# Batch 0's q in quarters and its k in pieces, k's maxima negated as they are written, identity products on TensorE, and a new order of all steps

## The chip, the cores and the metric

One core of a Trainium2 chip runs the kernel. Its engines work side by side, each through its own list of instructions in order: TensorE (PE for matmuls, PEld for loading their weights), VectorE (DVE), ScalarE (ACT), GpSimd (POOL), and SyncE (SP), which here issues every DMA. The metric is the device time of one execution in microseconds (us); less is better.

## The reference

Eight batches go through a linear attention and a gated MLP. Cut to what matters:

```python
q_s = softmax(q, axis=-1)              # q, k, v: (8 batches, 8 heads, 576 rows, 64)
k_s = softmax(k, axis=2)               # over the 576 rows
x   = q_s @ (k_s^T @ v)                # heads side by side: (8, 576, 512)
h   = gelu_tanh(x @ w_in)              # 512 -> 1024
u, v2 = h[..., :512], h[..., 512:]
v_n = (v2 - mean) / sqrt(var + 1e-6) * g_ln
v_s = w_sg @ v_n + b_sg                # over the 576 rows
out = x + (u * v_s) @ w_out
```

Both softmaxes take the maximum off before the exponential. w_in and w_out reach the device as 64-bit floating point.

## The kernel before, in words

All work is cut into named steps, one small Python function each. `PLAN` is one long text with about 1,270 steps such as `kv_mm 0 1` (batch 0, half 1) or `wi_a 3 G` (chunk 3, on GpSimd); the last loop of `gmlp_kernel` calls them in that order. `InOrder` chains each engine's instructions, so **each engine works through its own part of the plan strictly in order**, and so does SP with the DMAs. Engines meet only through data: a reader waits for the writer, and a writer into a buffer for its last reader. The planned order is thus the whole schedule, and a trailing letter (V, A, G) picks the engine.

A matmul on full fp32 would be slow, so each large operand is split in a high and a low part in the fp32r format, and a product is three matmuls (high x high, low x high, high x low).

- **Weights** (w_in in eight chunks `wi_* f`, w_out in four `wo_* f`): `load`, then `_a` (scale, ACT or POOL), `_b` (shift left by 3), `_c` (or the sign), `_d` (or the low word), all three on DVE, then `_h` (ACT rounds the high part) and `_l` (the low part). A low part comes either by a subtraction (DVE or POOL), or by `wi_x`, which lets TensorE form value minus high part with `eye` and `minus` (the identity and its negative) into PSUM, from where ACT copies it. w_sg goes the same way with `ws_h`, `ws_x`, `ws_l`.
- **k of a half of a batch**: for batch 0 it lies transposed (`TURN`), and `kr_max` takes the maxima over the rows with one reduction on DVE and negates them with a second small operation; `kr_exp` is the exponential on ACT, `ktr_mm` turns the result with ten transposes on TensorE, `kr_copy` and `kr_rest` bring it to `kk`. For the other batches `k_ma`, `k_mb`, `k_mc` fold the rows, further steps spread the maximum, `k_sub` and `k_exp` follow.
- **q of a half**: for batch 0 (`FLAT`) `qf_max`, `qf_sub`, `qf_exp`, `qf_sum`, `qf_inv` on a whole half, `qf_mul` on a quarter, then `qtr_mm` (transposes on TensorE) and `qf_copy` for each quarter. For the others `q_max`, `q_swapm`, `q_top`, `q_sub`, `q_exp`, `q_sum`, `q_swapd`, `q_inv`, `q_mul`, `q_turn` (a DVE transpose).
- **Attention**: `kv_mm` (k^T v), `kv_inv` and `kv_scale` (the division), `x_mm` (two of a batch), `x_high` and `x_low` (the split of x; in batch 0 some with `x_neg`, which takes the high part off in PSUM).
- **MLP**: `hu_mm` and `hv_mm` (x @ w_in for u and v; in batch 0 in two parts, `_first` and `_second`), `hu_gelu`, `hv_gelu`, `hv_sq`, `hv_stat`, `hv_pow`, `hv_norm`, `hv_high`, `hv_low`, the `tail_*` steps for the last 64 rows, `sg_mm` (the product over the rows), `gate`, `gate_high`, `gate_low`, `out_mm`, `out_base`, `out_add`, `out_store`. The last quarter of the last batch is halved in `last_mm`, `last_add`, `last_store`.

Buffers that steps share set waits: `kk`, `vv` and `qq` have one slot for each half, so `load_k b h` waits until `kv_mm b-1 h` has read the slot. PSUM has three two-bank tiles (`ps2`) and two one-bank tiles (`ps1`), handed out in turn by `bank` in the order of the plan.

Of the kernel before, what the change touches and what calls it, by code (L numbers as in the profile page):

```python
# [38 lines left out]
kv_inv 0 0, kv_scale 0 0, x_mm 0 0, x_high 0 0, wi_c 2, qf_mul 0 1 0 G, qtr_mm 0 2, wi_d 2, wi_h 2, load_w_in 7, wi_a 7 G, load_k 1 0, wi_b 7
load_k 1 1, wi_c 7, x_high 0 1, x_neg 0 0, wi_x 2, x_low 0 0 A, kv_inv 0 1, qf_copy 0 2, load_w_in 6, wi_b 1, k_ma 1 1, load_w_out 1, x_neg 0 1  # L40
x_low 0 1 A, k_ma 1 0, ws_x 3, wi_c 1, wi_a 6, k_mb 1 1, ws_l 3 A, kv_scale 0 1, x_mm 0 1, load_b, wi_d 1, wi_h 1, load_q 1 0, x_high 0 2, wi_b 6
load_q 1 1, k_mc 1 1, wi_c 6, wi_x 1, wi_l 1 A, k_mb 1 0, wi_d 7, x_neg 0 2, hu_first 0 0, wi_l 2 A, x_low 0 2 A, q_max 1 0, q_swapm 1 0, wi_h 7
wi_d 6, kt_mm 1 1, hu_first 0 2, x_high 0 3, k_mc 1 0, kt_mm 1 0, k_top 1 1, q_top 1 0, load_w_in 4, q_sub 1 0 G, q_max 1 1, kb_mm 1 1, k_top 1 0
x_low 0 3, hu_second 0 2, k_sub 1 1 V, hu_second 0 0, wi_a 4, wi_h 6, wi_l 7 G, b_h, load_w_in 5, wi_a 5, q_exp 1 0, hu_first 0 1, wi_b 5, wi_b 4
wi_c 5, wi_d 5, q_swapm 1 1, wi_c 4, q_top 1 1, q_sub 1 1 G, load_w_out 2, wi_h 5, load_v 1 1, load_w_out 3, kb_mm 1 0, k_exp 1 1, wi_d 4, wi_h 4
wi_x 6, wi_l 6 A, hu_second 0 1, k_sub 1 0 V, q_sum 1 0, wi_l 5 G, kv_mm 1 1, kv_inv 1 1, kv_scale 1 1, k_exp 1 0, q_swapd 1 0, load_v 1 0, kv_mm 1 0
wi_l 4 V, kv_inv 1 0, wo_a 2, load_w_sg 2, hv_first 0 3, hv_second 0 3, wo_a 3 G, b_l V, q_inv 1 0, kv_scale 1 0, q_exp 1 1, load_w_sg 1, hu_gelu 0 2
load_w_out 0, q_sum 1 1, q_mul 1 0 0 G, q_turn 1 0, hv_first 0 0, hv_gelu 0 3, wo_a 1, wo_b 1, wo_a 0, wo_b 3, wo_b 2, wo_c 3, hv_second 0 0, ws_h 1
q_mul 1 0 1 G, hv_gelu 0 0 A, load_w_sg 4, ws_h 2, wo_b 0, wo_c 0, wo_d 0, hu_gelu 0 0, hv_first 0 1, hv_second 0 1, q_turn 1 1, ws_h 4, wo_c 1
hv_gelu 0 1 A, wo_c 2, x_mm 1 0, wo_d 3, hu_gelu 0 1, q_swapd 1 1, wo_d 1, q_inv 1 1, q_mul 1 1 0 G, q_mul 1 1 1 G, hv_sq 0 1, load_v 2 0, x_high 1 0  # L50
wo_d 2, wo_h 2, wo_l 2 G, hv_first 0 2, hv_second 0 2, x_low 1 0, q_turn 1 2, hu_first 0 3, x_high 1 1, load_q 2 0, x_low 1 1, hv_sq 0 0, hv_first 0 4
ws_l 2 G, hv_gelu 0 2 A, hv_sq 0 2, q_turn 1 3, x_mm 1 1, load_g, hv_norm 0 1, x_high 1 2, hu_second 0 3, hv_stat 0 0 A, hv_pow 0 0, hv_stat 0 3
x_low 1 2, hv_stat 0 1 A, hv_pow 0 1, x_high 1 3, x_low 1 3, load_v 2 1, hv_pow 0 3, hv_norm 0 3, hv_high 0 3, hv_norm 0 0, hv_stat 0 2 A, hv_pow 0 2
hv_low 0 3, hv_high 0 0, hv_low 0 0, hv_second 0 4, hv_gelu 0 4 A, load_k 2 0, hv_sq 0 4, k_ma 2 0, k_mb 2 0, hv_high 0 1, ws_l 1 V, hv_mm 1 2
hv_gelu 1 2 A, hv_norm 0 4, hv_stat 0 4 A, hv_pow 0 4, hv_norm 0 2, load_k 2 1, hu_gelu 0 3, hv_low 0 1, k_ma 2 1, tail_high 0, tail_low 0, k_mc 2 0
k_fold 2 0, hv_sq 1 2, hv_high 0 2, hv_low 0 2, tail_high 1, tail_low 1, hv_mm 1 1, k_rota 2 0, k_maxa 2 0, load_q 2 1, k_rotb 2 0, q_max 2 1, wo_h 3
wo_l 3 G, hv_stat 1 2 A, tail_again 0, ws_l 4 V, out_base 0 2 G, wo_h 1, k_maxb 2 0, hv_mm 1 0, hv_gelu 1 0 A, hv_pow 1 2, sg_mm 0 2, q_max 2 0
hv_gelu 1 1, hv_stat 1 1, hv_norm 1 1, hv_pow 1 1, gate 0 2, q_swapm 2 0, q_swapm 2 1, hv_sq 1 0, q_top 2 1, q_sub 2 1 V, sg_mm 0 0, k_sub 2 0 V
sg_mm 0 1, k_exp 2 0, q_top 2 0, k_mb 2 1, gate 0 1, gate_high 0 2, q_sub 2 0 V, q_exp 2 0, gate 0 0, gate_high 0 0, gate_low 0 0 G, sg_mm 0 3
gate_high 0 1, gate_low 0 1 G, hv_norm 1 2, hv_high 1 2, kv_mm 2 0, k_mc 2 1, k_fold 2 1, q_sum 2 0, q_swapd 2 0, gate 0 3, gate_high 0 3, q_inv 2 0  # L60
gate_low 0 2 V, hv_mm 1 3, q_exp 2 1, gate_low 0 3 G, q_mul 2 0 1 G, wo_h 0, out_base 0 3 V, q_sum 2 1, hv_stat 1 0 A, wo_l 0 V, hv_gelu 1 3
hv_stat 1 3, hv_norm 1 3, q_swapd 2 1, q_inv 2 1, q_mul 2 1 1 G, q_turn 2 1, out_mm 0 2, out_add 0 2, q_mul 2 0 0 G, out_mm 0 3, out_mm 0 0
k_rota 2 1, q_mul 2 1 0 V, hu_mm 1 2, hv_pow 1 3, out_base 0 0 G, q_turn 2 3, kv_inv 2 0, k_maxa 2 1, kv_scale 2 0, k_rotb 2 1, q_turn 2 2
out_add 0 3, wo_l 1 G, k_maxb 2 1, out_add 0 0, hv_low 1 2, hv_pow 1 0, out_base 0 1 V, load_k 3 0, k_ma 3 0, out_mm 0 1, q_turn 2 0, hv_high 1 3
hv_low 1 3, hu_gelu 1 2, out_add 0 1, hu_mm 1 0, k_sub 2 1 G, k_exp 2 1, kv_mm 2 1, k_mb 3 0, k_mc 3 0, hv_high 1 1, hv_low 1 1, out_store 0 1
load_q 3 0, hu_gelu 1 0, x_mm 2 0, x_high 2 0, k_fold 3 0, k_rota 3 0, x_low 2 0, hv_norm 1 0, hv_high 1 0, hu_mm 1 1, q_max 3 0, hv_low 1 0
load_k 3 1, x_high 2 1, k_ma 3 1, out_store 0 2, x_low 2 1, hu_mm 1 3, k_mb 3 1, k_mc 3 1, kv_inv 2 1, kv_scale 2 1, hu_gelu 1 1, tail_again 1
k_fold 3 1, k_rota 3 1, load_q 3 1, q_max 3 1, out_base 1 1 V, q_swapm 3 0, k_maxa 3 1, sg_mm 1 0, load_v 3 0, k_maxa 3 0, k_rotb 3 0, k_maxb 3 0
k_rotb 3 1, k_maxb 3 1, k_sub 3 1 G, load_v 3 1, hu_gelu 1 3, out_base 1 2 V, k_exp 3 1, k_sub 3 0 V, k_exp 3 0, q_top 3 0, q_sub 3 0 G, gate 1 0
sg_mm 1 3, gate 1 3, out_store 0 0, gate_high 1 3, out_store 0 3, sg_mm 1 1, gate 1 1, gate_high 1 1, out_base 1 3 V, x_mm 2 1, gate_high 1 0  # L70
x_high 2 2, kv_mm 3 1, q_exp 3 0, out_base 1 0 G, gate_low 1 0 V, gate_low 1 1 V, kv_mm 3 0, x_high 2 3, x_low 2 3, q_sum 3 0, kv_inv 3 1
kv_scale 3 1, q_swapd 3 0, kv_inv 3 0, x_low 2 2, q_inv 3 0, q_mul 3 0 1 G, load_k 4 0, sg_mm 1 2, gate 1 2, q_swapm 3 1, gate_high 1 2, kv_scale 3 0
hv_mm 2 3, hv_gelu 2 3, q_turn 3 1, hv_mm 2 1, hv_gelu 2 1, q_top 3 1, q_sub 3 1 G, q_mul 3 0 0 G, q_turn 3 0, hv_stat 2 3, hv_pow 2 3, gate_low 1 2 V
gate_low 1 3 G, hv_mm 2 2, q_exp 3 1, q_sum 3 1, q_swapd 3 1, q_inv 3 1, q_mul 3 1 1 G, out_mm 1 1, out_add 1 1, load_q 4 0, hv_gelu 2 2 A, q_max 4 0
hv_sq 2 2, hv_norm 2 2, out_mm 1 0, q_swapm 4 0, q_top 4 0, x_mm 3 0, hv_stat 2 1, out_add 1 0, x_high 3 1, q_turn 3 3, q_sub 4 0 G, q_mul 3 1 0 G
q_turn 3 2, hv_mm 2 0, hv_gelu 2 0, x_high 3 0, x_low 3 0, x_low 3 1, out_mm 1 2, out_add 1 2, load_q 4 1, q_max 4 1, q_exp 4 0, hv_norm 2 3, x_mm 3 1
x_high 3 2, x_low 3 2, x_high 3 3, x_low 3 3, out_mm 1 3, q_swapm 4 1, k_ma 4 0, out_add 1 3, hv_high 2 3, hv_low 2 3, hv_mm 2 4, hv_gelu 2 4
hv_stat 2 4, hv_pow 2 4, hv_pow 2 1, hv_norm 2 4, q_top 4 1, q_sub 4 1 G, q_exp 4 1, hv_norm 2 1, q_sum 4 0, tail_high 2, hv_high 2 1, tail_again 2
# [766 lines left out]
```

## Time and profile before

| what | value |
| --- | --- |
| median of 3 runs | 511.39 us (510.62 to 513.59) |
| the profiled execution's own time | 510.1 us |
| its span, first to last instruction | 508.3 us |
| mean granted TensorE clock | 0.998 |
| DMA | 49.01 MB, mean 96 GB/s |
| table loads on ACT | 34, 43.6 us |

The page gives each engine's busy time as a share of the span; the view by stages gives the same for stretches of time, which shows what paces each of them. In the timeline a row is start, duration, engine, line, operation, what it writes and reads, shapes, and in brackets the engine's idle time before it and what ended it. All instructions issued through `InOrder` have line 156, and all matmuls line 243, so rows are told apart by the names of the tiles: `ot_i` and `raw_*` belong to w_in's conversion, `x_lk` holds batch 0's k, `km` maxima of k, `qq` q, `kvt` the scaled k^T v, `ps` PSUM.

### The profile page before, as it was taken

The numbers are of one execution on the slowest core, as the hardware profiler recorded it, in microseconds if no ns is written. First come the engines' busy times: TensorE is split into PE (matmuls) and PEld (weight loads), VectorE is DVE, ScalarE is ACT, GpSimd is POOL, SyncE is SP. The second block draws the span as 40 slices with busy tenths as digits, with TensorE's granted clock in tenths as the row PEclk, the third lists the DMA queues.
The fourth block names the chain that finished last, engine by engine and source line by source line (L and its number), as shares of the span: only waits on it lengthen the run. The fifth ranks groups of instructions, "written<-read, shape, count | busy, mean of one in ns | idle before, by whom it ended". The sixth has DMA issues, their size and how long they took to land. (4 is left out here: it accounts for less than half of the span.)

```text
span 508.3 us, 9454 instructions
## 1 busy us (share of the span) xinstructions
PE 487.6 (96%) x3841; PEld 445.5 (88%) x3841; DVE 351.9 (69%) x622; ACT 287.5 (57%) x603; POOL 140.7 (28%) x114
## 2 busy tenths in 40 slices
...
GB/s 327 308 349 308 141 137 0 54 2 281 63 53 48 174 2 171 32 39 202 78 46 153 47 1 197 2 25 165 163 2 0 51 44 1 1 23 71 1 1 93
DMA packets 19055, 49.01 MB, mean 96 GB/s; under 512 B 1602, under 2 KB 8132, under 8 KB 19012
## 3 DMA queue, kind: packets, MB, share of 16 engines
...
q14 instruction: 13, 0.11, 0.1%
...
## 5 line engine op out<-in xcount | busy, mean ns | idle before, releaser
L156 POOL TENSOR_TENSOR rs<-ve,half 128x1 f32<-128x1 f32 x36 | 24.9, 698 | 159.2 <-DVE ve L156 155.9
L243 PE MATMUL ps<-ulow,wo_h 128*128 128x288 f32 x256 | 55.6, 296 | 1.2 <-POOL ulow L156 0.9
L243 PE MATMUL ps<-gh,wo_h 128*128 128x288 f32 x256 | 55.9, 297 | 0.1
L243 PE MATMUL ps<-gh,wo_l 128*128 128x288 f32 x256 | 55.4, 295 | 0.0
L243 PE MATMUL ps<-ws_h,vnh 128*128 128x288 f32 x256 | 55.2, 297 | 0.0
L243 PE MATMUL ps<-ws_h,vnl 128*128 128x288 f32 x256 | 54.9, 296 | 0.0
L243 PE MATMUL ps<-ws_l,vnh 128*128 128x288 f32 x256 | 54.9, 295 | 0.0
L156 ACT ACT_TABLE_LOAD x34 | 43.6, 1283 | 10.3 <-issue 4.3
L156 POOL TENSOR_TENSOR ulow<-u,gh 128x576 fp32r<-128x576 f32 x16 | 23.5, 1468 | 83.0 <-ACT gh L156 76.0
L243 PEld LDWEIGHTS ps<-gh,wo_h 128*128 128x128 f32 x256 | 41.7, 188 | 1.8 <-DVE o L156 1.0
L243 PEld LDWEIGHTS ps<-ws_h,vnh 128*128 128x128 f32 x256 | 41.6, 188 | 1.6 <-DVE u L156 0.9
L243 PEld LDWEIGHTS ps<-ulow,wo_h 128*128 128x128 f32 x256 | 41.3, 188 | 1.7 <-POOL ulow L156 1.2
L243 PEld LDWEIGHTS ps<-ws_h,vnl 128*128 128x128 f32 x256 | 41.3, 188 | 0.2 <-DVE vnl L156 0.2
L243 PEld LDWEIGHTS ps<-ws_l,vnh 128*128 128x128 f32 x256 | 41.3, 188 | 0.0
L243 PEld LDWEIGHTS ps<-gh,wo_l 128*128 128x128 f32 x256 | 41.2, 188 | 0.0
L243 PE MATMUL ps<-wi_h,x_l 128*128 128x512 f32 x144 | 40.7, 397 | 0.4 <-DVE x_l L156 0.4
L156 ACT CAST gh<-u 128x576 fp32r<-128x576 f32 x32 | 21.2, 671 | 35.4 <-DVE u L156 35.3
L156 DVE TENSOR_TENSOR u<-ps,u 128x576 f32<-128x576 f32 x32 | 23.7, 749 | 24.8 <-PE ps L243 23.0
L243 PE MATMUL ps<-x_h,wi_h 128*128 128x288 f32 x256 | 40.8, 299 | 0.0
L243 PE MATMUL ps<-wi_h,x_h 128*128 128x512 f32 x144 | 40.7, 398 | 0.0
L243 PE MATMUL ps<-wi_l,x_h 128*128 128x512 f32 x144 | 40.1, 394 | 0.0
L243 PE MATMUL ps<-x_l,wi_h 128*128 128x288 f32 x256 | 40.0, 296 | 0.0
...
## 6 DMA issues: line engine op xcount, KB each, us to landing
vv<-v SPq DMA_DIRECT2D x16, 650.0 KB, 8.1
...
```

What stands on the lines that cost most here:

```text
L156: ins = op(*args, **kw)
L243: tc.keep_in_program_order(nc.tensor.matmul(*args, **kw))
```

## The change

1. Batch 0's q is loaded and worked on in quarters: `load_q`, `qf_max`, `qf_sub`, `qf_exp`, `qf_sum`, `qf_inv` take a third argument, and the array `q_flat` is laid out so that a quarter is contiguous.
2. Batch 0's k is loaded in four pieces of 576 columns (before, two of 2 x 640, with the last 64 rows twice); `kr_max` and `kr_exp` take a piece. The reduction writes the maxima negated, and the second operation goes. The last transpose of `ktr_mm` has 64 columns, `kr_rest` copies 64 partitions, and the new `kr_zero` sets the rest of that slot to 0.
3. Five new steps `warm n` multiply the identity by itself twice each, into a `ps2` tile that nobody reads.
4. The plan has a new order from the first step to the last. Among the steps whose engine or kind changes: `wi_x` and `wi_l` of chunks 3 and 6, and `ws_x 3`, are gone, and their low parts are subtractions on POOL (wi) and DVE (ws); `wi_a 3`, `wi_a 7` and `wo_a 3` go from POOL to ACT; `b_l` goes to POOL; many `gate_low`, `out_base`, `q_mul`, `q_sub` and `k_sub` change between DVE and POOL, and many `hv_gelu`/`hv_stat` pairs take the other of their two ways to the variance. The order by kind of function on ACT has 28 changes between exponential and gelu, where it had 34.
5. `shift`, `zero` and `both` in `converter` are changed or new, but the plan calls them only as before.

The core of the diff (of the plan, the first lines and the last two):

```diff
-load_w_in 3, wi_a 3 G, wi_b 3, wi_c 3, load_k 0 0, kr_max 0 0, load_w_in 0, wi_a 0, wi_d 3, wi_h 3, load_eye, wi_b 0, load_q 0 1, wi_c 0, qf_max 0 1
-neg, kr_exp 0 0, wi_x 3, ktr_mm 0 0, load_w_sg 0, ws_h 0, wi_l 3 A, load_q 0 0, wi_d 0, wi_h 0, ws_x 0, load_k 0 1, qf_max 0 0, wi_x 0, kr_max 0 1
...
+load_q 0 1 1, qf_max 0 1 1, qf_sub 0 1 1 G, qf_exp 0 1 1, load_q 0 0 1, qf_max 0 0 1, qf_sub 0 0 1 G, load_q 0 0 0, qf_max 0 0 0, qf_sub 0 0 0 G
+load_k 0 0 1, kr_max 0 0 1, kr_exp 0 0 1, load_eye, warm 6, warm 5, warm 0, load_b, warm 7, kr_zero 0 1, qf_exp 0 0 1, b_h, qf_sum 0 1 1, load_q 0 1 0
+qf_exp 0 0 0, warm 11, qf_max 0 1 0, load_k 0 0 0, qf_inv 0 1 1, kr_max 0 0 0, kr_exp 0 0 0, ktr_mm 0 0, load_k 0 1 0, kr_max 0 1 0, qf_sum 0 0 1
+load_k 0 1 1, kr_max 0 1 1, qf_sub 0 1 0 G, qf_exp 0 1 0, qf_sum 0 1 0, qf_sum 0 0 0, kr_exp 0 1 0, qf_inv 0 0 1, load_w_in 2, load_v 0 0
+qf_inv 0 1 0, kr_exp 0 1 1, ktr_mm 0 1, qf_mul 0 0 1 V, b_l G, kr_copy 0 0, load_w_in 0, kr_rest 0 0, qf_mul 0 1 1 G, kr_copy 0 1, wi_a 0, qtr_mm 0 3
+wi_a 2, kr_zero 0 0, qf_inv 0 0 0, qf_mul 0 0 0 V, load_w_in 3, wi_b 0, kv_mm 0 0, qtr_mm 0 0, kr_rest 0 1, qf_mul 0 1 0 V, wi_c 0, qf_copy 0 3, neg
+wi_a 3, wi_b 3, qtr_mm 0 1, qf_copy 0 1, kv_inv 0 0, wi_b 2, kv_scale 0 0, load_w_in 1, qf_copy 0 0, wi_a 1, qtr_mm 0 2, x_mm 0 0, qf_copy 0 2
+load_v 0 1, kv_mm 0 1, wi_c 3, x_high 0 0, x_high 0 1, x_neg 0 1, wi_d 0, wi_h 0, load_k 1 0, wi_x 0, wi_d 3, load_w_sg 0, ws_h 0, wi_c 2, load_w_in 4
...
-out_base 7 2 V, out_mm 7 0, out_add 7 2, out_store 7 2, out_add 7 0, last_mm 7 0, last_mm 7 1, out_store 7 0, last_add 7 0, last_store 7 0
-last_add 7 1, last_store 7 1
+gate_low 7 2 V, gate_high 7 3, gate_low 7 3 V, out_mm 7 1, last_mm 7 0, out_base 7 1 G, out_add 7 1, out_store 7 1, last_add 7 0, last_store 7 0
+out_mm 7 0, out_add 7 0, out_mm 7 2, out_store 7 0, last_mm 7 1, out_base 7 2 G, out_add 7 2, out_store 7 2, last_add 7 1, last_store 7 1
...
+    def warm(n):
+
+        ps = bank(ps2, "warm", n)
+        for i in range(2):
+            mm(ps[:, i, 0:P], eye, eye, start=True, stop=True)
...
-    def kr_max(b, h):
+    def kr_zero(b, h):
+        G.memset(kk_s(b, h, at=h)[TL:P, ST], 0.0)
+
+    def kr_max(b, h, a):
         m = km_s(b, h, at=2 * b + h, shape=[P, 2])
-        V.tensor_reduce(out=m, in_=turned(b)[:, h, :, 0:S], axis=AX.X, op=ALU.max)
-        V.tensor_scalar(out=m, in0=m, scalar1=-1.0, scalar2=None, op0=ALU.mult)
-
-    def kr_exp(b, h):
-        t, m = turned(b)[:, h], km_s(b, h)
-        for a in range(2):
-            A.activation(t[:, a], t[:, a], AF.Exp, bias=m[:, a:a + 1])
+        V.tensor_reduce(out=m[:, a:a + 1], in_=turned(b, h, a), axis=AX.X, op=ALU.max, negate=True)
+
+    def kr_exp(b, h, a):
+        t = turned(b, h, a)
+        A.activation(t, t, AF.Exp, bias=km_s(b, h)[:, a:a + 1])
...
+    def qf_max(b, h, a):
+        V.tensor_reduce(out=qm_s(b, h, at=h, shape=[P, 2, 10])[:, a], in_=groups(b, h, a), axis=AX.X, op=ALU.max)
+
+    def qf_sub(b, h, a, E=G):
+        z = groups(b, h, a)
+        E.tensor_tensor(out=z, in0=z, in1=qm_s(b, h)[:, a, :, None].broadcast_to([P, 10, D]), op=ALU.subtract)
...
+    def qf_inv(b, h, a):
+        d = qd_s(b, h)[:, a]
         V.tensor_scalar(out=d, in0=d, scalar1=1e-9, scalar2=None, op0=ALU.add)
         V.reciprocal(out=d, in_=d)
```

More of the change, by code (lines that the diff above doesn't have):

```diff
@@ L39 @@
[L39 to L78, printed above, removed]
@@ L99 @@
-kv_inv 5 1, load_q 6 0, q_max 6 0, q_swapm 6 0, q_top 6 0, out_base 3 1 V, load_k 6 0, kv_scale 5 1, hv_norm 4 1, q_sub 6 0 V, q_exp 6 0, out_mm 3 0
-q_sum 6 0, q_swapd 6 0, load_k 6 1, out_add 3 3, k_ma 6 1, k_mb 6 1, k_mc 6 1, out_add 3 0, out_mm 3 1, out_add 3 1, hv_mm 4 0, k_fold 6 1, out_mm 3 2
-out_add 3 2, hv_gelu 4 0, hv_stat 4 0, hv_stat 4 1 A, hv_pow 4 1, x_mm 5 0, x_high 5 0, hv_mm 4 2, x_low 5 0, k_rota 6 1, x_high 5 1, x_low 5 1
-x_mm 5 1, x_high 5 3, x_high 5 2, q_top 6 1, q_sub 6 1 G, q_exp 6 1, hu_mm 4 0, x_low 5 2, hv_norm 4 3, hv_high 4 3, hv_low 4 3, x_low 5 3, hu_mm 4 1
@@ L115 @@
-x_high 6 1, x_high 6 0, x_low 6 0, load_q 7 1, load_v 7 1, x_low 6 1, q_mul 7 0 1 V, hv_high 5 0, hv_low 5 0, k_ma 7 0, k_mb 7 0, out_store 4 1
-load_k 7 1, k_ma 7 1, k_mc 7 0, k_fold 7 0, hu_mm 5 1, kv_inv 6 1, k_mb 7 1, k_mc 7 1, q_max 7 1, kv_scale 6 1, hu_mm 5 0, hu_gelu 5 0, hu_gelu 5 1
-sg_mm 5 0, gate 5 0, gate_high 5 0, x_mm 6 1, x_high 6 3, x_high 6 2, x_low 6 2, out_base 5 1 V, sg_mm 5 1, hu_mm 5 2, gate 5 1, k_fold 7 1
-k_rota 7 1, out_base 5 2 V, x_low 6 3, hv_mm 6 1, hv_gelu 6 1 A, k_maxa 7 1, hv_sq 6 1, hv_norm 6 1, q_swapm 7 1, k_rotb 7 1, q_top 7 1
@@ new lines @@
+wi_a 2, kr_zero 0 0, qf_inv 0 0 0, qf_mul 0 0 0 V, load_w_in 3, wi_b 0, kv_mm 0 0, qtr_mm 0 0, kr_rest 0 1, qf_mul 0 1 0 V, wi_c 0, qf_copy 0 3, neg
+wi_a 3, wi_b 3, qtr_mm 0 1, qf_copy 0 1, kv_inv 0 0, wi_b 2, kv_scale 0 0, load_w_in 1, qf_copy 0 0, wi_a 1, qtr_mm 0 2, x_mm 0 0, qf_copy 0 2
+load_v 0 1, kv_mm 0 1, wi_c 3, x_high 0 0, x_high 0 1, x_neg 0 1, wi_d 0, wi_h 0, load_k 1 0, wi_x 0, wi_d 3, load_w_sg 0, ws_h 0, wi_c 2, load_w_in 4
+wi_a 4, k_ma 1 0, ws_x 0, kv_inv 0 1, wi_l 0 A, wi_b 1, x_neg 0 0, kv_scale 0 1, wi_h 3, wi_l 3 G, wi_c 1, wi_d 2, wi_h 2, wi_x 2, wi_d 1, wi_h 1
```

227 lines of the change are left out of this document (137 added, 90 removed).

## The prediction

> **What bounds the kernel now.** I read the page's busy line first, then the table by stages, then the timeline of each engine at the places where one stage hands over to the next.
>
> ```profile
> PE 487.6 (96%) x3841; PEld 445.5 (88%) x3841; DVE 351.9 (69%) x622; ACT 287.5 (57%) x603; POOL 140.7 (28%) x114
> ```
>
> The span is 508.3 us and the profiled execution took 510.1, so 1.8 lie around it; the median of the runs, 511.39, is 1.3 above that. Changes are reckoned against 510.1 and then put on 511.39. About 0.5% (2.6 us) is what a measurement of this kernel can tell from no change. By this line alone PE is the bound. The stages say more (columns: busy time of PE, PEld, DVE, ACT, POOL, the granted clock, DMA share, GB/s):
>
> ```profile
> core 0 of [0], span 508.3 us
> core 0: us, PE busy (x) PEld busy (x) DVE busy (x) ACT busy (x) POOL busy (x), PEclk, DMA share, GB/s
> 6.00:20.00 14.00, 8.98 (x32) 6.01 (x32) 13.71 (x17) 10.21 (x16) 6.13 (x4) 1.00 1.04 391
> 20.00:40.00 20.00, 18.70 (x199) 15.14 (x200) 18.86 (x36) 17.42 (x35) 5.87 (x4) 1.00 0.93 315
> 40.00:77.30 37.30, 36.86 (x270) 29.14 (x268) 35.35 (x71) 31.69 (x72) 15.89 (x15) 1.00 0.52 180
> 77.30:200.00 122.70, 121.72 (x971) 112.45 (x970) 101.99 (x175) 79.52 (x175) 44.64 (x31) 1.00 0.25 87
> 200.00:300.00 100.00, 97.49 (x822) 90.04 (x821) 71.80 (x133) 61.24 (x128) 33.32 (x24) 1.00 0.22 78
> 300.00:504.10 204.10, 203.83 (x1555) 192.74 (x1553) 109.40 (x193) 86.12 (x182) 30.88 (x30) 1.00 0.14 51
> ```
>
> DVE is busy 13.71 of 14 us before 20, 18.86 of the next 20, 35.35 of the next 37.3. PE is idle before 20 and full afterwards, but its order follows what DVE delivers. At 77.3 the first spatial-gate step (sg_mm 0 2) starts; its last products wait for DVE's residual of the last w_sg slice (ws_l 4):
>
> ```profile
> 80.43 0.81 DVE L156 TENSOR_TENSOR ws<-ghws,ws 64x640 fp32r<-64x640 f32 x1
> ```
>
> ```profile
> 81.39 0.50 PE L243 MATMUL ps<-ws,vn 128*128 128x288 f32 x2 [0.46 <-DVE ws L156]
> ```
>
> Behind 77.3 PE stands still for 0.98 + 2.51 + 0.27 = 3.8 us in 426.8. So **the sum is: when does the first sg step come, plus 426.8 us of PE, plus what changes in those 3.8 us and in the tail.** In both orders the same steps stand behind the first sg step, but for which quarter of batch 1's v half (hv_mm 1 0 or 1 3) is still to do.
>
> **The start.** The first kv_scale of batch 0 is the mark that I follow; before, it ends at 24.45 + 0.29 = 24.74:
>
> ```profile
> 24.25 0.17 DVE L156 RECIPROCAL kr<-kr 128x2 f32<-128x2 f32 x1
> 24.45 0.29 DVE L156 TENSOR_TENSOR kvt<-ps,kr 128x128 f32<-128x128 f32 x1
> ```
>
> Arrivals: the first load (0.524 MB) ended POOL's wait at 4.49, and the stage before 20 moves 0.391 MB per us. A q quarter has 0.328 MB, so the first comes about (0.524 - 0.328)/0.391 = 0.5 earlier, at 3.9, the next at 4.7 and 5.6, the k pieces (0.295 MB) at 6.3, 8.1, 8.9, 9.6, the fourth quarter at 7.3, w_in 2 at 11.0, v at 12.7, w_in 0 and 3 at 14.0 and 15.4. The queue is never empty there (DMA share 1.04), so of the moved loads only bytes count: the identity's 0.066 MB and the bias's 2.5 KB are lost in it.
>
> ```profile
> 4.49 1.52 POOL L156 TENSOR_SCALAR ot_i<-raw_vnl 128x512 f32<-128x512 f32 x1 [1.40 <-DMA raw_vnl<-w_in]
> 11.80 5.00 POOL L156 TENSOR_TENSOR qq<-qq,qm 128x1280 f32<-128x1280 f32 x2 [5.79 <-DVE qm L156]
> ```
>
> DVE per operation:
>
> ```profile
> L156 DVE TENSOR_REDUCE qm<-qq 128x20 f32<-128x1280 f32 x2 | 3.0, 1479 | 0.0
> L156 DVE TENSOR_REDUCE km<-x_lk 128x2 f32<-128x1152 f32 x2 | 2.7, 1344 | 0.0
> ```
>
> ```profile
> 6.04 0.43 DVE L156 TENSOR_SCALAR ot_i<-ot_i 128x512 uint32<-128x512 uint32 x1 [6.04 <-POOL ot_i L156]
> 6.50 0.69 DVE L156 SCALAR_TENSOR_TENSOR ot_i<-raw_vnl,ot_i 128x512 uint32<-128x512 uint32 x1
> ```
>
> ```profile
> 15.00 1.82 DVE L156 TENSOR_SCALAR km<-km 128x2 f32<-128x2 f32 x1
> 16.74 1.47 DVE L156 TENSOR_REDUCE qd<-qq 128x20 f32<-128x1280 f32 x1
> 18.24 0.18 DVE L156 TENSOR_SCALAR qd<-qd 128x20 f32<-128x20 f32 x1
> 18.45 0.28 DVE L156 RECIPROCAL qd<-qd 128x20 f32<-128x20 f32 x1
> 18.77 0.83 DVE L156 TENSOR_TENSOR qq<-qq,qd 128x640 f32<-128x640 f32 x1
> ```
>
> The two reductions give 1.05 ns an element and 0.13 fixed: 0.80 for a q quarter, 0.74 for a k piece. The negation inside the reduction I take as free (no row shows it; between 0 and 0.18 each, the small scalar operation above). In the new order DVE starts at 3.9 instead of 6.04, waits some 0.4 for arrivals, has the last k maximum at 12.2, the last sum at 13.8, and then three qf_inv (0.46 each) and three multiplications (0.83), with wi_b 0 and wi_c 0 (0.43 and 0.69) between, to 18.8; wi_b 3, kv_inv (0.3), wi_b 2 and kv_scale end at **20.3** if nothing holds DVE.
>
> Two things may. First, the negation of 15.00 took 1.82 and ended with POOL's two subtractions (11.80 + 5.00), where a like one took 0.18: a small scalar operation of DVE that meets POOL at work waits for POOL. The reductions beside it kept their 1.47. The change takes that operation away, but brings qf_inv 0 1 1 next to POOL's four quarter subtractions: 0 to 1.3 (half of POOL's 2.5). I take 0.6. [...]
>
> Second, ACT: the last k exponential ends at 12.95, then ktr_mm 0 1, its copy, and six short operations to wi_a 3.
>
> ```profile
> L156 ACT ACTIVATE x_lk<-x_lk,km 128x640 f32<-128x640 f32 x4 | 3.1, 816 | 0.8 <-DVE km L156 0.8
> L156 ACT ACTIVATE qq<-qq 128x1280 f32<-128x1280 f32 x2 | 2.5, 1264 | 0.0
> L156 ACT COPY kk<-ps 128x1024 f32<-128x1024 f32 x2 | 2.0, 1017 | 0.4 <-PE ps L243 0.4
> ...
> L156 ACT ACTIVATE ot_i<-raw_vnl 128x512 f32<-128x512 f32 x1 | 0.7, 707 | 0.0
> ```
>
> ```profile
> 9.31 2.07 PE L243 MATMUL ps<-ot_i,eye 128*128 128x512 f32 x2 [9.31 <-DVE ot_i L156]
> ```
>
> ```profile
> 11.61 2.33 PE L243 MATMUL ps<-eye,x_lk 128*128 128x128 f32 x10
> ```
>
> ```profile
> 18.45 1.21 PE L243 MATMUL ps<-eye,x_lk 128*128 128x128 f32 x9 [0.39 <-ACT x_lk L156]
> ```
>
> Ten transposes took 2.33 at 11.61, 2.3 us after PE's first product; nine took 1.21 at 18.45. With the fast group: 12.95 + 1.2 + 1.0 + 3 x 0.7 + three shorter ones (1.3, by their elements) = 18.5, before DVE needs it; with the slow one 19.6, and the mark moves by 0.8. The ten identity products begin when the identity lands (6.5), so ktr_mm 0 1 is 6.4 us behind the first product, nearer to the fast row; I take that. They read only the identity, nobody waits for them, and PE has nothing else then: cost 0, at most 0.8 if their bank turns were late.
>
> So the mark comes at **20.9** (20.3 to 22.4) instead of 24.74: 3.8 earlier. From it to ws_l 4 DVE's list is 0.3 longer (three conversions of 0.69 and the q of batch 2 change sides, b_l goes to POOL and ws_l 1 too, wo_l 1 and ws_l 3 come): **3.5 earlier** at the first sg step. PE must follow, as it is busy 36.86 of 37.3 there: it has two wi_x and one ws_x less ahead.
>
> ```profile
> 27.56 1.02 PE L243 MATMUL ps<-ot_i,eye 128*128 128x512 f32 x2
> 28.02 0.80 PE L243 MATMUL ps<-wi_h,minus 128*128 128x512 f32 x1
> 28.65 0.42 PE L243 MATMUL ps<-x_h,minus 128*128 128x288 f32 x2
> ```
>
> A wi_x takes 28.65 - 27.56 = 1.1, a ws_x by its columns (1920 to 1536) 1.4, together 3.6 less; enough for the 3.5. Beyond that it brings nothing. The subtractions that replace them go to POOL (wi_l 3, wi_l 6) and DVE (counted). load_k 1 0, which waits for kv_mm 0 0, moves with it; SP's loads behind it come earlier too. kr_zero is one small memset on POOL, hidden.
>
> **The tail.** Now both halves of the last addition run after the last product:
>
> ```profile
> 504.15 0.82 DVE L156 TENSOR_TENSOR o<-ps,o 128x288 f32<-128x288 f32 x2 [2.60 <-PE ps L243]
> ```
>
> In the new order last_mm 7 0 and its addition stand three steps earlier: 0.4 off. Sum: -3.5 - 0.4 = **-3.9**: 506.2 for a profiled execution, **507.5** as median. The engine swaps of batches 2 to 7 and six table loads fewer lie on engines with gaps; I cost them at nothing, and the 3.8 us of late stops as unchanged. Without that cover they are the rivals.
>
> **Rivals.** (1) *The late stops go too*: at most the 3.8, 503.7. For it: ACT is lighter. Against: nothing says which stop goes. (2) *DVE stays late in batch 3*:
>
> ```profile
> 167.49 0.47 PE L243 MATMUL ps<-qt,kvt 64*64 64x288 f32 x4
> ```
>
> ```profile
> 164.38 0.78 DVE L156 STREAM_TRANSPOSE qt<-qq 128x576 f32<-128x576 f32 x1 [1.05 <-POOL qq L156]
> ```
>
> x_mm 3 1 starts at 167.5, its last turn ended at 165.2. The new order takes 6.0 us of PE (hv_mm 2 2, out_mm 1 1) from before it, and only 2.3 of DVE. With DVE's waits unchanged, the turn ends at 162.9, while PE comes at 167.5 - 3.5 - 6.0 = 158.0: 4.9 lost, 512.4. For it: k_ma 4 0 and 4 1 now stand ahead of the turns. Against: many of DVE's waits there are for PE. (3) *Slower: the k loads*. In the new order k_ma 5 0 and k_ma 7 1 follow their load at once, and the load waits for the batch before's kv_mm. Before, such a load beside others landed in
>
> ```profile
> 351.43 8.19 DMA kk<-k
> ```
>
> and a lone load of that size in
>
> ```profile
> vv<-v SPq DMA_DIRECT2D x1, 650.0 KB, 3.8
> ```
>
> Behind k_ma 5 0 wait out_add 2 1 and so out_mm 2 0: 9.6 us of out_mm hide the landing and 4.2 of DVE, so it costs from 5.4 on. Behind k_ma 7 1 wait gate 5 0, x_low 6 1 and a turn for x_mm 6 1: 8.1 us of PE against 3.2, from 4.9 on. At 8.19 that is 2.8 + 3.3, with 0.6 at k_ma 4 0: 6.7 lost, **514.3**. Against: there the loads are alone in SP's order. [...]
>
> **Chances.** Forecast 0.45, (1) 0.18, (2) 0.15, (3) 0.10, (4) 0.12. The forecast's own bounds are 506.9 to 509.0 by the mark, half a us wider by the other unknowns (the negation, up to 0.7, among them). 508.8 and 513.9 are the limits of "same": faster is three quarters of the forecast, all of (1) and half of (4): 0.58; same 0.31; slower 0.11, mostly (3). The range 503.0 to 512.8 leaves out (3) and the edges of (1) and (2).
>
> **What would show it.** kvt's first write at 20.3 to 22.4; no TENSOR_SCALAR on km; the 640-column residual ws near 77; the first sg step near 74; PE idle behind it near 3.8; one 288-column addition after the last product. A stop ahead of x_mm 3 1, or k_ma waiting for kk, shows (2) or (3). If the mark is early and the first sg step is not, PE or ACT, not DVE, paced that stretch and the sum is wrong there.

## The result, and the profile after

| | before | after |
| --- | --- | --- |
| median | 511.31 us (510.62 to 513.59, 4 runs) | 504.65 us (503.76 to 505.44, 4 runs) |
| ratio, 95% interval | | 0.9862 [0.9824, 0.9899] |
| span of the profiled execution | 508.3 us | 502.0 us |

The forecast was 507.5 as a median. What was gained is 6.7 us of median and 6.3 of span, where 3.9 were forecast. First the busy line of the page, then the table by stages with the prediction's columns, cut where the first product of the MLP (31.3) and the first sg step (73.47) begin and where PE's last product ends (498.63):

```profile
PE 485.0 (97%) x3849; PEld 446.3 (89%) x3849; DVE 349.5 (70%) x620; ACT 280.5 (56%) x603; POOL 153.4 (31%) x126
```

```profile
6.00:20.00 14.00, 11.05 (x100) 10.10 (x100) 12.49 (x27) 12.18 (x22) 7.33 (x9) 1.00 1.02 354
20.00:31.30 11.30, 9.55 (x93) 5.67 (x94) 10.36 (x22) 9.70 (x19) 1.27 (x1) 1.00 1.04 388
31.30:73.47 42.17, 42.04 (x314) 35.46 (x314) 40.47 (x81) 38.46 (x89) 22.13 (x16) 1.00 0.60 216
73.47:200.00 126.53, 125.47 (x1006) 116.69 (x1005) 110.20 (x185) 82.84 (x191) 45.38 (x31) 1.00 0.23 80
200.00:300.00 100.00, 99.25 (x816) 90.90 (x816) 70.36 (x125) 57.76 (x128) 26.58 (x22) 1.00 0.29 101
300.00:498.63 198.63, 197.68 (x1526) 187.45 (x1525) 103.54 (x181) 78.28 (x159) 47.05 (x38) 1.00 0.12 42
498.63:502.00 3.37, 0.00 (x0) 0.00 (x0) 0.46 (x1) 0.00 (x0) 0.00 (x0) 1.00 0.36 134
```

From 31.3 on PE has hardly a gap. The rows of the timeline that answer to those of before: DVE's first operation, the first write of kvt, the residual of the last w_sg slice, the last addition.

```profile
3.80 1.63 DVE L158 TENSOR_REDUCE qm<-qq 128x10 f32<-128x640 f32 x2 [3.80 <-DMA qq<-q_flat]
...
20.02 0.28 DVE L158 TENSOR_TENSOR kvt<-ps,kr 128x128 f32<-128x128 f32 x1
...
75.71 0.81 DVE L158 TENSOR_TENSOR ws<-ghws,ws 64x640 fp32r<-64x640 f32 x1
...
498.67 0.46 DVE L158 TENSOR_TENSOR o<-ps,o 128x288 f32<-128x288 f32 x1 [0.77 <-PE ps L245]
```

So kvt is written at 20.3 instead of 24.74, and ws_l 4 ends at 76.5 instead of 81.2, just before PE asks for it (76.68). **The difference of the spans in three parts:**

| part | before | after | gain | forecast |
| --- | --- | --- | --- | --- |
| first sg step comes at | 77.30 | 73.47 | 3.8 | 3.5 |
| from there to PE's last product | 426.75 | 425.15 | 1.6 | 0 |
| from PE's last product to the end | 4.28 | 3.37 | 0.9 | 0.4 |

PE's stops behind the first sg step were 3.8 us before (the prediction's windows) and are 1.06 + 0.75 + 0.95 = 2.8 now. None stands where one stood before. The three of any size, in the timeline of PE:

```profile
142.57 0.63 PE L245 MATMUL ps<-vv,kk 128*64 128x65 f32 x14 [0.93 <-ACT v L158]
...
237.35 0.53 PE L245 MATMUL ps<-ws_h,vnl 128*128 128x288 f32 x2 [0.68 <-DVE vnl L158]
...
405.16 0.53 PE L245 MATMUL ps<-x_h,wi_h 128*128 128x288 f32 x2 [0.95 <-ACT u L158]
```

The first and the last follow a gelu on ACT that frees a PSUM bank, and ACT loads the table for it just before, after idle time of its own (1.89 and 7.46 us):

```profile
140.41 1.28 ACT L158 ACT_TABLE_LOAD   x1 [1.89 <-PE ps L245]
...
403.16 1.28 ACT L158 ACT_TABLE_LOAD   x1 [7.46 <-PE ps L245]
```

### The profile page after: what moved, and what is told of

Same layout as the page of the kernel before. It is cut to its first block, busy times and chain, and to the rows that moved or that the text cites. A ratio compares the mean times of both kernels' runs of the same rounds, so it can differ in the third digit from the quotient of the medians.

```text
span 502.0 us, 9486 instructions
## 1 busy us (share of the span) xinstructions
PE 485.0 (97%) x3849; PEld 446.3 (89%) x3849; DVE 349.5 (70%) x620; ACT 280.5 (56%) x603; POOL 153.4 (31%) x126
## 4 chain that ended last, share of the span: by engine, by line
PE 85%; ACT 6%; DMA 4%; DVE 3%; issue 1%; POOL 1%; SPq 0%; ACTq 0%
PE ps L245 85%; DMA raw_wo_h<-w_in 1%; DMA kk<-k 1%; DMA x_lk<-k_turn 1%; DVE qd L158 1%; ACT L158 1%; DMA qq<-q_flat 1%; ACT qq L158 1%; DVE km L158 1%; ACT v L158 1%; ACT kk L158 0%; ACT u L158 0%; ACT gh L158 0%; ACT sq L158 0%; ACT wi_h L158 0%
## 5 line engine op out<-in xcount | busy, mean ns | idle before, releaser
L158 POOL TENSOR_TENSOR rs<-ve,half 128x1 f32<-128x1 f32 x36 | 27.3, 764 | 91.9 <-DVE ve L158 91.6
L158 POOL TENSOR_TENSOR ulow<-u,gh 128x576 fp32r<-128x576 f32 x15 | 21.9, 1462 | 93.6 <-ACT gh L158 75.1
```

Source lines behind the costliest of these rows:

```text
L158: ins = op(*args, **kw)
```

## The experiments

**The theory to be tested:** the three parts add, and the first is set by DVE's list up to ws_l 4. Ratios are always to the kernel before.

### The new start with the old order behind it, twice

The plan of the new kernel up to k_fold 2 0, and what is not done by then in the order of before (the place where one order takes over from the other is called the seam below):

```diff
 k_mb 2 0, k_mc 2 0, k_fold 2 0
-tail_again 0, hv_low 0 2, tail_low 0, hv_mm 1 3, hv_gelu 1 3 A, wo_l 1 V, ws_l 3 V, hv_mm 1 1
+ws_l 3 V, wo_l 2 G, load_v 2 1, tail_low 0, hv_low 0 2, tail_high 1, tail_low 1, hv_mm 1 1
...
```

> The new kernel with its own order up to the folding of batch 2's first k half (k_fold 2 0, some 65 us), and from there the order and the engine letters of before. Theory A (start, middle and tail add up: the first sg step came 3.8 us earlier, PE behind it took 1.6 less, the work after PE's last product 0.9 less): only the 3.8 stays, 511.3 - 3.8 = 507.5, first sg step near 73.5, PE idle behind it near the 3.8 of before. Rival B (the early start is worth something only with the new order behind it, since DVE or ACT is late again by 130): within 1 us of before, 510.3 to 512.3. Rival C (the order behind the start brings nothing of its own): as the new kernel, 504.7.

Measured: 510.45 us, ratio 0.9985 [0.9969, 1.0002]. The first sg step came at 73.9, but PE stopped in it for 0.78 and 2.71 us. In the timeline:

```profile
79.82 1.32 DVE L158 TENSOR_TENSOR ws<-ghws,ws 64x640 fp32r<-64x640 f32 x1
...
81.29 0.51 PE L245 MATMUL ps<-ws,vn 128*128 128x288 f32 x2 [2.71 <-DVE ws L158]
```

ws_l 4 ended at 81.14, as late as before (81.24). Ahead of it the old order has one q maximum of batch 2 (1.34 us; the expectation below counts two, but the other runs behind it, at 82.85) and other steps, and ws_l 4 itself took 1.32 instead of 0.81 us while POOL was at work. The time is what rival B names, so the seam was moved behind ws_l 4:

```diff
 hv_mm 1 1, k_rotb 2 1, ws_l 4 V
-sg_mm 0 2, hv_sq 1 3, k_rota 2 0, k_maxa 2 0
+wo_l 2 G, load_v 2 1, tail_high 1, tail_low 1, k_rota 2 0, k_maxa 2 0, load_q 2 1, k_rotb 2 0, q_max 2 1
...
```

> As start_new, with the seam behind the new order's last w_sg residual (ws_l 4), right ahead of sg_mm 0 2, so that DVE's list ahead of that residual is the new kernel's; from there the order and letters of before. Theory A (DVE's list up to ws_l 4 decides the first sg step, and start_new lost 3.5 only because the old order put two q maxima ahead of ws_l 4): ws_l 4 ends near 76.5, no stop of more than 0.5 in sg_mm 0 2, and 511 - 3.8 = 507.2 (507.5 against 511.3). Rival B (the old order behind gives an early start back at its next wait, wherever the seam lies): 510 or more, with a stop of 2 to 3 us somewhere before 240.

Measured: 507.8 us, ratio 0.9927 [0.9905, 0.9948], 3.7 us (2.7 to 4.9) less than before; ws_l 4 ended at 76.87 (76.06 + 0.81), and sg_mm 0 2 had no stop. Its first sg step came at 76.22, because this mixed plan has all four quarters of hv_mm ahead of it, where both kernels have three; the fourth took PE from 73.33 to 76.22.

```profile
75.33 0.82 DVE L158 TENSOR_TENSOR ws_l<-ghws,ws_h 128x640 fp32r<-128x640 f32 x1
76.06 0.81 DVE L158 TENSOR_TENSOR ws<-ghws,ws 64x640 fp32r<-64x640 f32 x1
```

So **by the medians the start alone is worth 3.7, and nearly all of it is lost where ws_l 4 comes late on DVE**. Between the two kernels only the place of the seam differs. The size is less sure than the place: the two profiled executions differ by only 2.0 (spans 508.3 and 506.3), and in start_sg PE stood still for 5.1 us behind the first sg step, 1.4 more than before.

### The old start with the new order behind it, twice

The plan of before up to k_fold 2 0 (late_new), or up to the step ahead of sg_mm 0 2 (late_sg, whose edit is shown), and what is not done by then in the order of the new kernel:

```diff
 hv_mm 1 0, hv_gelu 1 0 A, hv_pow 1 2
-sg_mm 0 2, q_max 2 0, hv_gelu 1 1
+k_mb 2 1, k_mc 2 1, k_fold 2 1, k_rota 2 1, k_maxa 2 1, hv_mm 1 3, hv_gelu 1 3 A, wo_l 1 V, k_rotb 2 1, sg_mm 0 2
...
```

> The counterpart: the kernel before with its own start up to k_fold 2 0, and from there the order and the engine letters of the new kernel. Theory A: the first sg step stays at 77.3 and the 1.6 + 0.9 go, 511.3 - 2.5 = 508.8. Rival B (the new order behind needs an early start): 511 or more. Rival C (all is won in the start): 511.3.

> As late_new, with the seam right ahead of sg_mm 0 2 of the kernel before: the start of before, the order and letters of the new kernel behind it. Theory A (middle and tail add 1.6 + 0.9 whatever the start is): 511 - 2.5 = 508.5. Rival B (the new order needs DVE to be as early as its own start makes it; late_new lost 1.7 in sg_mm 0 2, 1.4 in batch 2's kv_mm and out_mm and 0.6 more at sg_mm 3 0): 510.5 to 512, with stops behind sg_mm 0 2 of over 5 us in sum.

Measured: 512.4 us, ratio 1.0032 [1.0014, 1.0049], and 516.85, ratio 1.012 [1.008, 1.016]. Theory A fell in both: they are slower than before. In the first, sg_mm 0 2 waits 1.71 for hv_low on DVE:

```profile
81.45 0.53 PE L242 MATMUL ps<-ws_h,vnl 128*128 128x288 f32 x2 [1.71 <-DVE vnl L155]
```

In the second, PE waits 3.96 us for batch 2's k, and then something new shows in the stages (the granted clock is the third column from the right; 1.00 is full speed):

```profile
96.99 1.24 PE L242 MATMUL ps<-vv,kk 128*64 128x65 f32 x18 [3.96 <-ACT kk L155]
```

```profile
93.00:94.93 1.93, 0.03 (x1) 0.00 (x0) 1.93 (x1) 1.69 (x3) 1.28 (x1) 1.00 0.00 0
94.93:101.75 6.82, 4.76 (x81) 4.64 (x82) 4.43 (x11) 5.51 (x9) 4.03 (x3) 0.50 0.17 53
```

After 1.9 us without a product, still inside the gap, the granted clock falls to 0.50, for 6.82 us. What the new order of the later batches is worth without its own start stays open: both seams leave DVE behind and measure that.

### The tail

```diff
-out_mm 7 1, last_mm 7 0, out_base 7 1 G, out_add 7 1, out_store 7 1, last_add 7 0, last_store 7 0
-out_mm 7 0, out_add 7 0, out_mm 7 2, out_store 7 0, last_mm 7 1, out_base 7 2 G, out_add 7 2, out_store 7 2, last_add 7 1, last_store 7 1
+out_mm 7 2, out_base 7 1 G, out_mm 7 1, out_add 7 1, out_store 7 1, out_base 7 0 V, out_base 7 3 G, out_base 7 2 V, out_mm 7 0
+out_add 7 2, out_store 7 2, out_add 7 0, last_mm 7 0, last_mm 7 1, out_store 7 0, last_add 7 0, last_store 7 0, last_add 7 1, last_store 7 1
```

> The new kernel with only the steps behind hu_gelu 7 2 (the last 24 or so) in the order of before. Theory A (the last addition has one half instead of two behind PE's last product, and one last store stands behind it instead of two): 0.9 slower than the new kernel, 505.5, with two 288-column additions in a row at the end. As the prediction had it (the addition alone, 0.4): 505.1. Rival (the last store's way to memory hides it): 504.7.

Measured: 504.71 us, ratio 0.9876 [0.9854, 0.9898]; from PE's last product to the end 4.16 us, where the new kernel has 3.37. Over the profiles of this study the old tail took 3.86 to 4.27 (four kernels, mean 4.04), the new one 3.22 to 3.54 (ten, mean 3.35). So the profiles show 0.7; the times alone can't tell it from nothing.

### The identity products

```diff
         ps = bank(ps2, "warm", n)
-        for i in range(2):
-            mm(ps[:, i, 0:P], eye, eye, start=True, stop=True)
```

> The new kernel without the ten identity products (their five bank turns are kept). Leaves out only products that nobody reads. Theory A (they open the clock for the transposes of k): ktr_mm 0 0, ten transposes in 1.27 us in the new kernel, goes back to some 2.3, and ktr_mm 0 1 too; kr_copy 0 1 ends at 16.9 instead of 15.7, the first write of kvt comes at 21.1 to 21.5 instead of 20.3, and the time is 0.8 to 1.2 longer, 505.5 to 505.9. Rival B (slow transposes, but PE and ACT have room there and DVE sets the mark): ktr_mm 2.3 each, kvt at 20.3, 504.7. Rival C (the clock is the same with or without): ktr_mm 1.3, 504.7.

Measured: 505.42 us, ratio 0.9892 [0.9869, 0.9916]. The twenty transposes of k, without the products and with them (start_sg, same start):

```profile
11.34 4.53 PE L245 MATMUL ps<-eye,x_lk 128*128 128x128 f32 x20 [11.34 <-ACT x_lk L158]
```

```profile
11.18 3.01 PE L245 MATMUL ps<-eye,x_lk 128*128 128x128 f32 x20
```

Theory C is out as far as the durations go: without the products the transposes take 0.23 us each (4.53 for twenty), with them 0.15 (3.01). That the clock is the reason is not shown, since the profile gives a granted clock of 1.00 for those of 0.23 us too (11.34 to 15.90). kvt's first write ended at 20.44, where eight profiles with this start and the products have 19.01 to 20.31; the loss of 0.8 by the medians is within what the intervals leave open, so between A and B it is not settled.

### The negation

```diff
-V.tensor_reduce(out=m[:, a:a + 1], ..., op=ALU.max, negate=True)
+V.tensor_reduce(out=m[:, a:a + 1], ..., op=ALU.max)
+V.tensor_scalar(out=m[:, a:a + 1], in0=m[:, a:a + 1], scalar1=-1.0, scalar2=None, op0=ALU.mult)
```

> The new kernel with k's maxima negated by a second operation again, one behind each of the four maxima of a k piece. Theory A (a small scalar operation of DVE that meets POOL at work ends with POOL's operation): the four take their 0.17 each and wait for POOL's operations that end at 8.55, 10.79, 11.7 and 12.5, 1.5 to 2.5 in sum; the first write of kvt comes 1.5 to 2.5 later and the time is 1 to 2.5 longer, 505.7 to 507.2. Rival B (only their own 0.17 count): 0.7 later, 505.3. Rival C (DVE has room there): 504.7.

Measured: 503.94 us, ratio 0.9855 [0.9822, 0.9888]: as the new kernel. Theory A fell. The first of the four, and POOL's three subtractions beside it, which run without a pause until 8.43:

```profile
7.32 0.15 DVE L158 TENSOR_SCALAR km<-km 128x1 f32<-128x1 f32 x1
```

```profile
4.74 3.69 POOL L158 TENSOR_TENSOR qq<-qq,qm 128x640 f32<-128x640 f32 x3 [1.64 <-DVE qm L158]
```

No wait. Yet before's negation took 1.82 us. It had two columns, these have one, which led to the probe:

```diff
+    def pr(n):
+        V.tensor_scalar(out=spare[:, 0:n], in0=qm_s(0, 1)[:, 1, 0:n], scalar1=-1.0, scalar2=None, op0=ALU.mult)
...
-load_q 0 0 1, qf_max 0 0 1
+load_q 0 0 1, qf_max 0 0 1, pr 1, pr 3, pr 2, pr 3
...
-kr_max 0 0 1
+kr_max 0 0 1, pr 3, pr 10, pr 1
```

> The new kernel with seven small scalar operations on DVE beside POOL's first subtractions: of 1, 3, 2 and 3 columns behind qf_max 0 0 1, of 3, 10 and 1 behind kr_max 0 0 1, into a spare tile that nobody reads. Before's negation had 2 columns, took 1.82 us and ended with POOL's operation; the four of 1 column in neg_apart took 0.15 with POOL at work. Theory A (an even number of columns makes the operation wait for the end of the POOL operation in progress): those of 2 and 10 columns end with a POOL operation, those of 1 and 3 take 0.15. Rival B (more than one column makes it wait): those of 3 wait too. Rival C (before's wait was of another kind, for its data): all take 0.15 to 0.18.

Measured (one time, 507.05 us). The groups of these operations by shape, and two of POOL's subtractions beside them:

```profile
L158 DVE TENSOR_SCALAR spare<-qm 128x3 f32<-128x3 f32 x3 | 1.5, 491 | 0.1
L158 DVE TENSOR_SCALAR spare<-qm 128x2 f32<-128x2 f32 x1 | 1.2, 1182 | 0.0
...
L158 DVE TENSOR_SCALAR spare<-qm 128x10 f32<-128x10 f32 x1 | 0.3, 344 | 0.0
L158 DVE TENSOR_SCALAR spare<-qm 128x1 f32<-128x1 f32 x2 | 0.3, 150 | 0.0
```

```profile
4.79 2.48 POOL L158 TENSOR_TENSOR qq<-qq,qm 128x640 f32<-128x640 f32 x2 [1.69 <-DVE qm L158]
8.29 1.26 POOL L158 TENSOR_TENSOR qq<-qq,qm 128x640 f32<-128x640 f32 x1 [1.02 <-DVE qm L158]
```

```profile
8.79 0.78 DVE L158 TENSOR_SCALAR spare<-qm 128x3 f32<-128x3 f32 x1
```

Three columns at 8.79 took 0.78 and ended at 9.57, POOL's subtraction at 9.55; a three-column operation that met POOL idle took 0.17 in the same trace. Rival B holds for the shapes tried (1, 2, 3 and 10 columns): **with two or more columns the operation waited for POOL's operation in progress (1.18 us with two, 0.78 with three, 0.34 with ten, where the ten of qf_inv 0 1 1 take 0.16 in a pause of POOL in the new kernel), with one it did not (0.15).** The reductions did not stretch: in the new kernel the one at 7.86, beside POOL's subtractions (4.76 to 8.55), took 0.81 us, and the one at 3.80, of the same 640 elements, 0.82 before POOL began.

### Less work for PE in the start

```diff
-wi_x 2
...
-wi_x 1, wi_l 1 A, load_k 1 1, wi_l 2 A
+wi_l 1 G, load_k 1 1, wi_l 2 G
```

> The new kernel with wi_x 1 and wi_x 2 (two products of 1.09 us each on TensorE, and ACT's copies of 0.6 behind them) replaced by subtractions of 1.27 us on POOL, which has nothing to do from 15 to 27. Theory A (behind 31 PE sets the pace in the new kernel, 42.04 busy of 42.17 us, and DVE's last w_sg residual is only half a us behind it): the first sg step comes 1 to 2 us earlier, the last products of sg_mm 0 2 wait up to 1.5 for ws_l 4, and 0.4 to 0.8 are won, 504.0. As the prediction had it (DVE sets the first sg step, less work on PE brings nothing): 504.7, ws_l 4 at the same time as in the new kernel. Rival (POOL's subtractions come too late for the first MLP products): hu_first 0 1 later than 31.3, 505.5.

Measured: 506.07 us, ratio 0.9904 [0.9867, 0.994]: nothing won. Here too the granted clock fell, inside a gap of 2.40 us:

```profile
28.10 2.20 PE L245 MATMUL ps<-qt,kvt 64*64 64x288 f32 x16 [2.40 <-ACT x_l L158]
```

```profile
25.70:27.66 1.96, 0.00 (x0) 0.00 (x0) 0.51 (x1) 1.96 (x5) 1.58 (x2) 1.00 1.03 401
27.66:34.49 6.83, 6.36 (x34) 4.95 (x35) 6.73 (x13) 4.30 (x10) 2.91 (x3) 0.50 1.06 371
```

That seemed the cause, and the next kernel keeps the products of wi_x 1 and wi_x 2, so that PE has no such gap:

```diff
-wi_l 1 A, load_k 1 1, wi_l 2 A
+wi_l 1 G, load_k 1 1, wi_l 2 G
```

> As pe_less (the low parts of w_in 1 and 2 by POOL's subtraction), but with the six products of wi_x 1 and wi_x 2 still made on TensorE, into PSUM that nobody reads any more. Theory A (what cost pe_less its time is the clock: PE stood still for 2.4 us ahead of x_mm 0 1, and the records show 0.50 of the clock from 27.66 to 34.49 behind it, 6.83 us at half rate): with the products kept the stop is under 1.5 us, the clock stays at 1.00, and the first sg step comes 1 to 1.5 us earlier than in pe_less counted from x_mm 0 1, as in the new kernel: ratio to before 0.986, 504.5. Rival B (POOL's subtractions are late or hold up DVE): as pe_less, 506.

Measured: 505.94 us, ratio 0.9902 [0.9874, 0.9929]. The clock stayed at 1.00 and the first MLP product came at 29.8 instead of 31.3, but the first sg step only at 74.7 (pe_less 74.4, the new kernel 73.5). Theory A fell: with the clock open nothing was won either. Between those two points PE now stood still for 2.0 us, where the new kernel has 0.1. What holds it is in the timeline:

```profile
27.70 2.88 POOL L158 TENSOR_TENSOR wi_l<-ot_i,wi_h 128x512 fp32r<-128x512 f32 x2
...
28.07 1.38 DVE L158 TENSOR_TENSOR km<-km,kk 128x256 f32<-128x256 f32 x1
...
29.37 1.50 DVE L158 TENSOR_SCALAR ot_i<-ot_i 128x512 uint32<-128x512 uint32 x1
...
33.98 0.44 PE L245 MATMUL ps<-eye,km 128*128 128x128 f32 x2 [1.44 <-DVE km L158]
```

The two DVE operations take 0.42 and 0.43 elsewhere; beside POOL's subtractions they took 2.0 us more together, and PE then waited 1.44 for DVE's maxima. Here DVE paid for the work that went to POOL. What fewer products on PE would bring without that is not shown by either kernel.

### Halves in place of quarters and pieces

```diff
-load_q 0 1 1, qf_max 0 1 1, qf_sub 0 1 1 G, qf_exp 0 1 1, load_q 0 0 1, qf_max 0 0 1
+load_q 0 1, qf_max 0 1, qf_sub 0 1 G, load_q 0 0, qf_max 0 0, qf_exp 0 1, qf_sub 0 0 G, load_k 0 0, kr_max 0 0
...
```

> The new kernel with batch 0's q and k loaded and worked on in halves again (one DMA, one maximum, one subtraction, one exponential, one sum for each half of q, one DMA and one maximum for each half of k), the start's steps up to ktr_mm 0 1 put in order by hand, everything behind in the new order. Theory A (most of the start's gain comes from what stands first, q and k ahead of w_in's conversion, and from DVE's small operation that no longer waits for POOL; cutting to pieces only lets DVE start some 0.8 earlier): the first maximum at 4.7 instead of 3.8, the first write of kvt 0.5 to 1.5 later than in the new kernel, 505.2 to 506.2. Rival B (the cutting is the gain, since a half passes DVE, POOL, ACT and DVE one behind the other): kvt at 23 or later, 507.5 or more.

Measured: 505.87 us, ratio 0.9896 [0.9877, 0.9914].

```profile
4.95 3.12 DVE L156 TENSOR_REDUCE qm<-qq 128x20 f32<-128x1280 f32 x2 [4.95 <-DMA qq<-q_flat]
...
20.82 0.28 DVE L156 TENSOR_TENSOR kvt<-ps,kr 128x128 f32<-128x128 f32 x1
```

kvt's write ends at 21.1, 0.8 later than in the new kernel, and the median is 1.2 longer, as theory A has it, though the two intervals overlap. The first sg step comes at 74.1, still 3.2 earlier than before. So most of the start's gain is there without the cutting. That it comes from the order of the steps is argued: no run undoes that order and keeps the rest.

### The three late stops

```diff
+    def pre():
+        A.activation(spare[:, 0:1], half, AF.Gelu_apprx_tanh)
...
-k_exp 3 1
+k_exp 3 1, pre
...
-hv_low 3 2, k_maxa 5 1, hu_mm 3 0, q_inv 5 0, hv_low 3 1
+hv_low 3 2, hv_low 3 1, k_maxa 5 1, hu_mm 3 0, q_inv 5 0
...
-k_exp 7 0
+k_exp 7 0, pre
```

> The new kernel with its three late stops taken up: a gelu of 128x1 into a spare tile directly behind k_exp 3 1 and behind k_exp 7 0, so that ACT loads its table in time in which it idles, and hv_low 3 1 ahead of k_maxa 5 1 on DVE. Theory A (the stops of 0.93 ahead of kv_mm 3 1 and 0.95 ahead of hu_mm 6 1 are the table loads of 1.28 behind which a gelu frees a PSUM bank; that of 0.68 in sg_mm 3 0 is DVE's order): all three under 0.2, PE idle behind the first sg step 0.5 instead of 2.7, 2.2 less than the new kernel, 502.4. Rival B (what goes there comes back at the next wait for DVE): 504.0 or more, with new stops.

Measured: **501.33 us** (500.37 to 502.09), ratio 0.9805 [0.9783, 0.9827]: faster than both kernels, its slowest run below the fastest of the new one (503.76). The table load now stands in ACT's idle time, and PE's stages behind the first sg step (73.86) are full:

```profile
136.88 1.28 ACT L159 ACT_TABLE_LOAD   x1
138.17 0.20 ACT L159 ACTIVATE spare<-half 128x1 f32<-128x1 f32 x1
...
140.75 0.60 ACT L159 ACTIVATE v<-ps 128x512 f32<-128x512 f32 x1 [1.46 <-PE ps L247]
```

```profile
73.86:200.00 126.14, 126.09 (x1011) 117.40 (x1010) 110.95 (x186) 83.71 (x193) 45.32 (x31) 1.00 0.23 81
200.00:300.00 100.00, 99.91 (x817) 91.29 (x816) 69.57 (x124) 58.32 (x132) 26.57 (x22) 1.00 0.29 101
300.00:496.15 196.15, 196.15 (x1521) 186.20 (x1519) 103.49 (x181) 77.28 (x155) 47.03 (x38) 1.00 0.12 42
```

PE's idle time there fell from 2.8 to 0.1, the stretch from the first sg step to PE's last product from 425.2 to 422.3, and the time by 2.9 (the two ratios, of 511.3): here the stops of PE behind the first sg step were paid in full, and taken away they did not come back. The three edits were made together, so this is their sum.

## Why the prediction was right, and where it was not

- **"The sum is: when does the first sg step come, plus 426.8 us of PE, plus what changes in those 3.8 us and in the tail."** It held. The eight kernels with the new order up to and behind the first sg step, and the late stops left in, took 424.8 to 425.7 us from there to PE's last product, while their first sg step lay anywhere from 72.96 to 76.54.
- **The start, -3.5.** Right in mechanism, and in size as far as it can be told: 3.8 in the profile, 3.7 by the medians of start_sg, but 2.0 between its profile and before's. DVE began at 3.80 (forecast 3.9), the mark came at 20.3 (20.9). The 0.6 taken for qf_inv 0 1 1 did not occur: it ran at 9.31 in 0.16, in the pause between POOL's third and fourth subtraction (8.55 to 9.53). A late ws_l 4 on DVE takes the gain away, as start_new shows. But in the new kernel PE, too, sets the first sg step: from the first MLP product at 31.3 it is busy for 42.04 of 42.17 us, and ws_l 4 ends only 0.16 before PE asks for it.
- **"A small scalar operation of DVE that meets POOL at work waits for POOL."** Right for the row it came from (1.82 us), and for the two, three and ten columns of the probe (1.18, 0.78, 0.34); wrong for one column (0.15). The negation's place in the reduction is free, as forecast (0.75 us a piece), but brings nothing either: with one column a piece, neg_apart is as fast. The removed wait was real for the two columns of before.
- **"Beyond that it brings nothing"** (PE's work in the start). Not settled. pe_less takes two more wi_x away and wins nothing, but its subtractions on POOL hold up DVE (1.38 us for km<-km,kk at 28.89, 0.42 elsewhere) and its granted clock falls (0.50 for 6.83 us), so the saving by itself was not tested.
- **The identity products.** Free, and on the fast side, as forecast. They began at 7.38, not 6.5, and ten products are twenty records that took 4.4 us up to the first transpose (11.81). They are products on full fp32, and such a product was slow here: before, one of 320 columns (two records) and one fp32r product of that width took 0.69 us together (28.91 to 29.60, ghws and ws_h), while the fp32r products of 288 columns followed each other every 0.13 us (33.76 to 35.35, twelve); by their columns that is an estimate of 0.54 for the one and 0.15 for the other.

```profile
7.38 4.64 PE L245 MATMUL ps<-eye 128*128 128x128 f32 x20 [7.38 <-DMA eye<-identity]
```

- **"The 3.8 us of late stops as unchanged."** This is the term that was mis-sized: its share of the gain is 1.6. Idle time fell by 1.0, and the same 3,348 products took 0.6 us less of busy time, for which no cause was found. Which change of the later order took the old stops away stays open too, since late_new and late_sg could not isolate it. What remained were new stops at new places, two of them behind table loads; best shows what all three together cost.
- **The tail, -0.4.** It was 0.9 in the profile. The sum counted the addition (ended 0.5 us after PE's last product instead of 0.9), but not that one last store, not two, stands behind it.
- **Rivals.** (1) went a quarter of its way. (2) did not occur: PE has no stop at batch 3's turns. (3) occurred in its first half: k_ma 5 0 and k_ma 7 1 waited 1.50 and 1.36 us for their loads, and no stop of PE follows. k_ma 5 1, which the rival does not name, waited longest,

```profile
231.15 0.69 DVE L158 TENSOR_TENSOR km<-kk 128x512 f32<-128x512 f32 x1 [2.63 <-DMA kk<-k]
```

and the 0.68 us stop in sg_mm 3 0 stands behind it in DVE's order, where the rival counted 6.7. (4), slow transposes of k that move the mark by 0.8 (0.12 of the chances), did not occur: the last nine transposes of k took 1.20 us, on the fast side. No run shows that a clock sets their time: in no_warm those of 0.23 us stand at a granted clock of 1.00.
